# A conditioned attention and spatial-shift block on one core: the opening reordered, modulation loads issued by SyncE, shift-column loads in steps, two tail subtractions later

## The chip, the cores and the metric

The kernel runs on one core of one Trainium2 chip. The metric is the device time of one execution in microseconds (us), as the median of several runs. Runs of the same program differ by some tenths of a per cent. A core has five engines that work side by side, each through its own list of instructions in a fixed order: TensorE (PE: matmuls and transposes, with PEld for its weight loads), VectorE (DVE), ScalarE (ACT), GpSimd (POOL) and SyncE (SP, which here only issues DMA transfers). ScalarE can issue DMA transfers too. An instruction waits until what it reads is written and the buffer it writes is free; everything behind it on the same engine waits with it.

## The reference, cut to what matters

```python
def _A_ref(x, wqkv, wo):                      # S 2048, D 576, 32 heads of 18
    q, k, v = split(x @ wqkv)
    scores = einsum("bhqd,bhkd->bhqk", q, k) * 18 ** -0.5
    scores = where(0 <= query - key < 256, scores, -1e9)
    return merge(einsum("bhqk,bhkd->bhqd", softmax(scores), v)) @ wo

def _B_ref(x, w1, w2, w3, w4):                # F 4608
    h = gelu(layernorm(x) @ w1)
    hs = concat(four column groups of h, shifted by +1, -1, +2, -2 tokens) @ w2
    x1 = x + hs
    return x1 + gelu(layernorm(x1) @ w3) @ w4

sa, ca, ga, sb, cb, gb = six vectors of 576 from silu(c) @ w_mod
h = layernorm(x) * (1 + ca) + sa
x = x + ga * _A_ref(h, A_wqkv, A_wo)
h = layernorm(x) * (1 + cb) + sb
x = x + gb * _B_ref(h, B_w1, B_w2, B_w3, B_w4)
```

All data is fp32. Each of the six vectors `sa` to `gb` is called a modulation vector below; number 0 and 1 (`sa`, `ca`) are needed at the start, 2 to 5 later.

## The kernel before, in words

**Matmuls in two halves.** A matmul with full fp32 meaning is made of products of a high part (the value rounded to the fast matmul type) and a low part (what the rounding left). For an inner size of 576, four blocks of 128 and a tail of 64, that gives 14 matmuls for one result (`products`). So each operand is "split": one engine copies the high half, another subtracts it from the original for the low half.

**Stages.** The 2048 tokens lie in four groups of 512. Group by group their rows are normalised (`x_load`, `x_norm`), transposed to features by tokens (`x_tr`: transpose L373, scale and shift on ScalarE L380, high half on GpSimd L383, low half on VectorE L387; the result is `hT`) and multiplied by nine chunks of 128 columns of the q and k weights (`qk_item`, one "item" of 14 matmuls at L398, evicted by ScalarE L419, split by GpSimd L423 and L427) and by the V weights (`v_item`). The halves of q and k are stored to DRAM by SyncE (L435 to L441).

Attention runs in 32 units `u` of four heads and 512 queries. `pack(u)` loads a unit's q and k halves back from DRAM with twelve DMAs on SyncE (L475, L478) into one of three buffers (the third is called `big`), 1.6 units ahead. `scores(u)` makes a first set of score matmuls (L492) from which VectorE takes the row maxima (L499); they are transposed, copied by ScalarE (L518) and written by a DMA of ScalarE (L519) as two more rows of `Q`. `attend(u)` makes the scores again, transposed and with the maximum taken off (L539, and L548 for the mask), ScalarE's exponential (L558) into `P`, and the product with V (L569); the result is stored to the DRAM array `od` (L604).

While attention still runs, `s4a` does the output projection of the finished groups: it loads rows of `od` (L845) and x (L849), transposes them (L854), multiplies by `Wo` (L888), adds (VectorE, L893), normalises, and stores `xp`, `hbd`, `xnd` (L905). `load_w1` loads and splits five chunks of the mixer's first weights; one of them, `W14`, gathers sixteen columns from each of eight places, and its raw rows `W14r` come by twelve small DMAs (L975). `xnt0` transposes the first rows for the mixer: transposes L782, high halves by ScalarE (L785 and, for the 64-row tail, L796), low halves by VectorE (L789, tail L800). After attention the mixer and the channel MLP (L1380, L1426) follow; the change does not touch them.

**Later modulation vectors.** `modvec(v)` makes vector 2 to 5 in turn, in time units 2.7, 7.7, 12.7 and 17.7 and the five units after each. It loads five slices of 576 columns of `w_mod` by DMAs that ScalarE issues (L623), each one unit apart; GpSimd scales and adds them (L630, L632); a matmul with ones (L638) sums them over the partitions, and VectorE evicts the result (L641); SyncE stores it to the DRAM array `modd` (L644). All four vectors use one buffer `wm`, so the first load of a vector reuses what the store of the vector before reads.

**What sets the order.** `play(ev)` takes a list of pairs of time and step, and runs the steps by rising time. The times are written by hand, in units `u`; they only set the order in which instructions are emitted, and each engine keeps that order. Negative times are the opening, before unit 0.

**The opening.** `warm` issues matmuls on zeros (L269). `c_load` and `cond` make silu of the condition; `wm_load` loads the five slices of `w_mod` for vectors 0 and 1 (SyncE, L263), `mod_sum` multiplies them (L278), and `mod_row`, `mod_tr`, `mod_col` turn the result into columns. `w_load` loads a chunk of q and k weights `wr` (L306, with two DMAs for the tail in `load_dup`, L116 and L117), `w_split` splits it (ScalarE L313 and L314, VectorE for the low half). `clear` and `vones` are memsets of Q, K and V buffers by GpSimd.

Of the kernel before, what the change touches and what calls it, by code (L numbers as in the profile page):

```python
# [9 lines left out]
F32 = mybir.dt.float32  # L10
F32R = mybir.dt.float32r
BF16 = mybir.dt.bfloat16
AF = mybir.ActivationFunctionType
# [40 lines left out]
class Kern:  # L54
# [134 lines left out]
    def phase_a(self):  # L189
# [10 lines left out]
        with ExitStack() as st:  # L200
# [18 lines left out]
            def clear(i):  # L219
                nc.gpsimd.memset(Q[i].bitcast(F32), 0.0)  # L220
                nc.gpsimd.memset(K[i][96:128].bitcast(F32), 1.0)
# [76 lines left out]
            def w_load(c):  # L298
                def f():
                    raw = kp.tile([P, 1024], F32, tag="P", name=f"wr{c}", bufs=7)[:, 0:640] if c in (0, 4, 5, 1) else row(f"wr{c}")  # L300
# [3 lines left out]
                    if c == 0:  # L304
                        nc.vector.memset(raws[c][0:1, 0, 0:1], 0.0)
                    nc.sync.dma_start(raws[c][:, 0:KC, :], self.wqkv[0:KC * P, cs].rearrange("(k p) f -> p k f", p=P))  # L306
# [3 lines left out]
            def w_split(c, t, lo):  # L310
# [9 lines left out]
                return [(t, hi), (t + self.g_w, low)]  # L320
# [43 lines left out]
            def x_tr(g, k, t0):  # L364
# [3 lines left out]
                def tr():  # L368
                    if k == 0:
                        hT[g] = gp.tile([P, 2 * KC + 1, 512], F32R, tag="L", name=f"hT{g}", bufs=1)  # L370
                    pa = box["p"] = ps([P, 4, P], ("tr", "mm", "tr", "mm", "tr")[k] if g else ("mm", "tr", "av", "sc", "st")[k], f"hT{g}_{k}")
# [3 lines left out]
                def ev():  # L375
# [4 lines left out]
                    nc.scalar.activation(h[:n], box["p"][:n].rearrange("p a b -> p (a b)"), AF.Identity, bias=sa[:n, k:k + 1], scale=ca[:n, k:k + 1])  # L380
# [10 lines left out]
                return [(t0, tr), (t0 + 0.02, ev), (t0 + 0.055, hi), (t0 + 0.105, lo)]  # L391

# [221 lines left out]
            def modvec(v):  # L614
                acc = []

                def load(k):
                    def f():
# [4 lines left out]
                        nc.scalar.dma_start(acc[1 if k == 0 else 2][:kk], self.w_mod[k * P:k * P + kk, v * D:(v + 1) * D])  # L623
# [23 lines left out]
                return e + [(4.5 + 0.07 * hf + d, f) for hf in range(2) for d, f in bcast(hf)]  # L647
# [41 lines left out]
            wt = {0: -8.975, 4: -8.974, 5: -8.973, 1: -8.7, 6: -7.45, 2: -1.9, 7: -1.5, 3: -1.2, 8: -0.9}  # L689
            first = {0: (-8.2, -8.0), 4: (-7.95, -7.75), 5: (-7.7, -7.5), 1: (-2.08, -1.75), 6: (-1.08, -0.98), 2: (0.05, 0.4), 7: (0.9, 1.2), 3: (1.35, 1.65), 8: (1.8, 2.1)}  # L690
            ev = [(-9.5, warm(24)), (-9.45, consts), (-9.44, vones(0, 4)), (-9.405, c_load), (-9.2, wm_load), (-9.05, cond)]
            ev += [(-8.93, lambda: clear(1)), (-7.35, lambda: clear(2)), (-1.2, vones(4, 10))]
# [828 lines left out]
```

## Time and profile before

| | |
|---|---|
| runs of the kernel before | 1704.92, 1705.19 and 1711.11 us, median 1705.19 us |
| the profiled execution | 1705.17 us, with a span of 1703.4 us on the core and a mean granted TensorE clock of 0.993 |
| DMA | 283.04 MB in 160767 packets, 166 GB/s on average |
| costliest line | L1426, the last matmuls of the channel MLP: 440.7 us in 3036 matmuls, with 0.0 us idle before them |
| row maxima on VectorE (L499) | 270.8 us in 512 instructions of 544 ns on average |
| exponentials on ScalarE (L558) | 217.1 us in 384 instructions of 571 ns on average |

The profile is of one execution. A row of a trace list reads: start in us from the beginning of the span, length in us, engine, line, operation, output<-input by the program's names, and in brackets the idle time just ahead of it with what ended it (`<-ACT P L558` is the instruction of ScalarE at line 558 that writes or frees `P`). `SPq` and `ACTq` are the queues of SyncE and ScalarE in which DMA issues stand; the length of such a row is the time that the issue took. `xN` stands for N instructions in a row. A row of the list of waits reads: engine, what it wants, line, the releaser, then total us, number and the longest. A row of a window reads: from and to, length, then busy us and number of instructions of PE, PEld, DVE, ACT and POOL, the granted clock (1.00 is full speed), the DMA engines' busy share and GB/s.

### The profile page before, as it was taken

The page shows a single profiled execution, that of the slowest core. Times are in us where ns is not written, and L with a number is a line of the kernel's source. Part 1 is how long each engine was busy: PE and PEld are TensorE (multiplying, and loading weights), DVE is VectorE, ACT ScalarE, POOL GpSimd, SP SyncE. Part 2 cuts the span into 40 slices and gives each one's busy share as a digit, 9 for nine tenths or more (in the row PEclk, how much of TensorE's full clock was granted, in tenths as well). Part 3 has the DMA queues.
Part 4 walks back from the last instruction along what each step waited for, and adds up shares of the span by engine and source line. Part 5 has one row for each costly group of instructions (what it writes and reads, how often), then busy time and mean ns, then how long its engine had stood idle before and what let it go on. Part 6 is the DMA issues. An engine that isn't in the chain of part 4 may idle for free.

```text
span 1703.4 us, 30698 instructions
## 1 busy us (share of the span) xinstructions
PE 1648.5 (97%) x11103; PEld 1428.6 (84%) x11103; DVE 1176.5 (69%) x2527; ACT 710.0 (42%) x1324; POOL 803.8 (47%) x790
## 2 busy tenths in 40 slices
PE   8999899999998999999999999999999999999999
PEld 5777688777777787888999999999999999999998
DVE  5665565665676774777787888888875666666667
ACT  3354354554555665534244344343434222222221
POOL 6323232231335553134188888888864333323335
PEclk8999999999999999999999999999999999999999
DMA  7644545534557774544455655556565544455443
GB/s 201 204 125 148 137 122 139 151 110 121 146 161 195 194 199 144 186 127 139 145 193 189 223 203 195 177 208 225 207 218 185 173 157 139 135 170 173 136 137 110
DMA packets 160767, 283.04 MB, mean 166 GB/s; under 512 B 37988, under 2 KB 77412, under 8 KB 160616
## 3 DMA queue, kind: packets, MB, share of 16 engines
q1 hardware_dynamic: 157672, 275.24, 51.9%
q10 hardware_dynamic: 2944, 5.83, 1.3%
q8 instruction: 88, 1.44, 0.4%
q14 instruction: 63, 0.52, 0.1%
HBM read 168.71 MB, written 111.63 MB: 165 GB/s over the span
## 4 chain that ended last, share of the span: by engine, by line
PE 81%; DVE 6%; DMA 6%; POOL 3%; ACT 2%; issue 1%; SPq 1%; ACTq 0%; POOLq 0%; DVEq 0%
PE pall L1380 27%; PE pall L1426 24%; PE pall L398 8%; PE pall L569 4%; PE pall L539 4%; PE pall L492 4%; PE pall L548 2%; PE pall L811 2%; PE pall L888 2%; PE pall L1164 2%; DVE pall L499 1%; DMA Q<-ms 1%; DMA wr<-in_A_wqkv_dram 1%; PE pall L580 1%; DMA modd<-wm 0%
## 5 line engine op out<-in xcount | busy, mean ns | idle before, releaser
L1426 PEld LDWEIGHTS pall<-W,G 128*128 128x128 f32 x3036 | 428.3, 188 | 19.2
L1426 PE MATMUL pall<-W,G 128*128 128x288 f32 x3036 | 440.7, 294 | 0.0
L499 DVE CUSTOM_DVE_ANT_0 pall<-pall,mask 128x384 f32<-128x384 f32 (+2 forms) x512 | 270.8, 544 | 194.9 <-PE pall L492 191.8
L1380 PE MATMUL pall<-LNT,W 128*128 128x512 f32 x1512 | 374.8, 390 | 0.0
L1435 DVE TENSOR_TENSOR accA<-pall,accA 128x576 f32<-128x576 f32 (+1 forms) x337 | 254.1, 756 | 120.8 <-PE pall L1426 109.3
L1351 POOL TENSOR_TENSOR g<-g,g 128x512 f32<-128x512 f32 x140 | 185.6, 1326 | 292.3 <-DVE G L1346 150.1
L1380 PEld LDWEIGHTS pall<-LNT,W 128*128 128x128 f32 x1512 | 274.7, 188 | 45.5
L558 ACT ACTIVATE P<-pall 128x512 f32<-128x512 f32 (+2 forms) x384 | 217.1, 571 | 180.8 <-PE pall L548 160.4
L1343 ACT CAST G<-g 128x512 fp32r<-128x512 f32 x249 | 151.1, 621 | 271.7 <-POOL g L1351 269.9
L1346 DVE TENSOR_TENSOR G<-g,G 128x512 fp32r<-128x512 f32 x249 | 240.7, 968 | 11.5 <-ACT G L1343 11.4
L1384 ACT ACTIVATE g<-pall 128x512 f32<-128x512 f32 x144 | 85.9, 596 | 194.3 <-PE pall L1380 184.7
L1435 DVE TENSOR_TENSOR accB<-pall,accB 128x576 f32<-128x576 f32 x134 | 101.3, 757 | 91.1 <-PE pall L1426 89.1
L398 PE MATMUL pall<-hT,Wc 128*128 128x512 f32 x504 | 158.8, 416 | 3.7 <-POOL hT L383 1.6
L423 POOL CAST qe<-qe 128x512 fp32r<-128x512 f32 x36 | 22.7, 630 | 244.8 <-ACT qe L419 232.4
L492 PE MATMUL pall<-K,Q 108*128 108x384 f32 (+2 forms) x352 | 125.7, 368 | 2.3 <-DVE m L499 0.8
L1380 PE MATMUL pall<-big,W 128*128 128x512 f32 x504 | 126.2, 390 | 0.0
L548 PE MATMUL pall<-maskb,identb 128*128 128x256 bf16 (+1 forms) x640 | 121.0, 255 | 0.0
L539 PE MATMUL pall<-Q,K 110*128 110x384 f32 (+1 forms) x480 | 105.7, 293 | 6.0 <-DMA Q<-ms 3.1
L1380 PEld LDWEIGHTS pall<-big,W 128*128 128x128 f32 x504 | 90.9, 188 | 14.1
L539 PEld LDWEIGHTS pall<-Q,K 110*128 110x128 f32 x480 | 86.3, 192 | 19.1 <-issue 6.1
L398 PEld LDWEIGHTS pall<-hT,Wc 128*128 128x128 f32 x504 | 86.7, 192 | 16.7 <-issue 3.3
L398 PE MATMUL pall<-Wv,hT 128*128 128x288 f32 x448 | 83.8, 311 | 2.7 <-ACT qe L419 2.7
(679 smaller groups left out, 2399.8 us busy)
## 6 DMA issues: line engine op xcount, KB each, us to landing
w4d<-W SPq DMA_DIRECT2D x55, 576.0 KB
W<-w4d SPq DMA_DIRECT2D x55, 576.0 KB
w3d<-W SPq DMA_DIRECT2D x36, 640.0 KB
W<-w3d SPq DMA_DIRECT2D x36, 640.0 KB
r<-in_B_w_dram SPq DMA_DIRECT2D x36, 288.0 KB
K<-k0d SPq DMA_DIRECT2D x64, 108.0 KB
Q<-q0d SPq DMA_DIRECT2D x88, 72.0 KB
w4d<-W SPq DMA_DIRECT2D x17, 288.0 KB
```

The source lines that it names most:

```text
L398: nc.tensor.matmul(pm, pl()[i][0], pl()[i][1], start=(i == 0), stop=(i == 13))
L492: nc.tensor.matmul(sc[:, lo:], q[0:2 * R3, h, i * P:(i + 1) * P], k[0:2 * R3, h // 2, i * P + lo:(i + 3) * P], start=True, stop=True)
L499: nc.vector.tensor_tensor_reduce(out=sc[:, lo:], in0=sc[:, lo:], in1=mask[:, lo:], scale=1.0, scalar=-3e38, op0=ALU.add, op1=ALU.max, accu ...
L539: nc.tensor.matmul(x[:, p0 * P:(p0 + w) * P], k[0:2 * R3 + 2, h // 2, (kb + 2) * P:(kb + 3) * P], q[0:2 * R3 + 2, h, q0 * P:(q0 + w) * P], ...
L548: nc.tensor.matmul(x[:, p0 * P:(p0 + w) * P], self.identb, m, start=False, stop=(n == len(ms) - 1))
L558: nc.scalar.activation(pt[:, c0:c1, h % 2, :], x[:, c0 * P:c1 * P].rearrange("p (a b) -> p a b", b=P), AF.Exp, scale=SCALE)
L1343: nc.scalar.copy(T[:, 0], src())
L1346: nc.vector.tensor_tensor(out=sp[m][:, 1], in0=src(), in1=sp[m][:, 0].bitcast(F32), op=sub)
L1351: nc.gpsimd.tensor_tensor(out=g[o] if o in g else gt(o), in0=g[a], in1=g[b], op=op)
L1380: nc.tensor.matmul(box["p"], box["l"][i][1], box["l"][i][0], start=(i == 0), stop=(i == 13))
L1426: nc.tensor.matmul(po, a, b, start=(n == 0), stop=(n == len(seq) - 1))
L1435: nc.vector.tensor_tensor(out=ac, in0=po, in1=ac, op=ALU.add)
```

## The change

It has five parts.

1. *Opening.* 36 instead of 24 warm-up matmuls. The transposes of the first group's rows are issued row by row (`x_tr0(i)`: the five blocks of row i), between the `mod_sum` steps, instead of block by block after them; scaling and splitting stay by block. The split of weight chunk 0 moves behind the first block's high half, and its low half follows it with a lag of 0.002. Chunk 4's load gets a wait: ScalarE copies one element of the fourth slice of the modulation weights into its buffer first, so that it (and chunk 5 behind it) starts when that slice is there. Chunks 6 and 2 get buffers of the `P` kind and are loaded right behind chunk 1, not among the q and k stores and loads. The last two products of item 0 (chunk 0) are put late, behind the first six of item 4. The clears of the second and third Q and K buffers, and six of the memsets of V, come later.
2. *Modulation loads.* `modvec`'s loads are issued by SyncE instead of ScalarE, and everything of `modvec` starts 0.6 units earlier, the summing matmul 0.05 of a unit more.
3. *Shift columns.* The twelve DMAs of `W14r` come in five steps 0.2 of a unit apart: pairs for the four blocks of 128 rows, four DMAs for the tail. The split of all five W1 chunks stands 1.2 units after the first DMA instead of 0.8 (`w1_d`).
4. *Tail low halves.* In `xnt0` the low halves by VectorE come at 0.17 and 0.21 instead of 0.1 and 0.16.
5. The lag of `w_split` becomes an argument, with the same default of 0.05.

What stands in ScalarE's order around the first load of the second later vector (`wm` is its buffer, `avs` an eviction of `attend`), before:

```order
L558 ACTIVATE P_0_0_2138<-pall 128x4x128 x2
L574 COPY avs_2184<-pall 128x512
L558 ACTIVATE P_0_2_2186<-pall 128x4x128
L623 DMA wm_2195<-in_w_mod_dram 128x576
L558 ACTIVATE P_0_2_2186<-pall 128x4x128
L419 COPY qe_3_2206<-pall 128x512
```

And the same load in SyncE's order, with the change (L623 is now the store to `od`, L663 the store to `modd`, L642 the modulation load, L458 and L460 k stores, L494 and L497 the loads of a unit's q and k):

```order
L623 DMA od_129<-o_2031 128x4x72
L663 DMA modd_133<-wm_1133 1x576
L642 DMA wm_2086<-in_w_mod_dram 128x576
L458 DMA k0d_147<-qe_7_2070 128x512
L460 DMA k0d_149<-qe_7_2070 128x256
L458 DMA k1d_148<-qe_7_2070 128x512
L460 DMA k1d_150<-qe_7_2070 128x256
L494 DMA Q_170<-q0d_139 18x2x512
L497 DMA K_172<-k0d_147 18x2x768
```

The load has left ScalarE's exponentials; on SyncE it stands right behind the store that it waits for, with four stores of k and the next unit's twelve loads behind it.

SyncE's order at the loads of the shift columns, before:

```order
L604 DMA od_131<-o_5647 128x4x72
L975 DMA W14r<-in_B_w_dram 128x4x16 x4
L975 DMA W14r<-in_B_w_dram 64x4x16 x2
L975 DMA W14r<-in_B_w_dram 128x4x16 x4
L975 DMA W14r<-in_B_w_dram 64x4x16 x2
L849 DMA s4rows<-in_A_x_dram 128x576
L905 DMA hbd_81<-or_5300 128x576
L475 DMA big<-q0d_143 18x2x512
```

With the change:

```order
L623 DMA od_131<-o_5660 128x4x72
L1005 DMA W14r<-in_B_w_dram 128x4x16 x2
L873 DMA s4rows<-in_A_x_dram 128x576
L1005 DMA W14r<-in_B_w_dram 128x4x16 x2
L929 DMA hbd_81<-or_5318 128x576
L1005 DMA W14r<-in_B_w_dram 128x4x16 x2
L494 DMA big<-q0d_143 18x2x512
```

Six of the twelve stand ahead of the unit's loads now, two of them behind the store of `hbd`; the other six follow behind the unit's loads.

VectorE's order in the tail of attention, before and then with the change (`big` holds the transposed rows for the mixer there, L893 and L917 are the add of the output projection, L789 and L812 the large low half, L800 and L823 that of the 64-row tail):

```order
L143 SCALAR_TENSOR_TENSOR b10rs<-b10mv,b10rs 128x1
L789 TENSOR_TENSOR big<-pall,big 128x4x128
L800 TENSOR_TENSOR big<-pall,big 64x128
L893 TENSOR_TENSOR s4rows<-pall,s4rows 128x288
L789 TENSOR_TENSOR big<-pall,big 128x4x128
L800 TENSOR_TENSOR big<-pall,big 64x128
```

```order
L143 SCALAR_TENSOR_TENSOR b10rs<-b10mv,b10rs 128x1
L812 TENSOR_TENSOR big<-pall,big 128x4x128
L917 TENSOR_TENSOR s4rows<-pall,s4rows 128x288
L823 TENSOR_TENSOR big<-pall,big 64x128
L812 TENSOR_TENSOR big<-pall,big 128x4x128
```

The add has passed the first of the 64-row pieces; the large piece still stands ahead of it.

The diff, cut to what the text above and the prediction speak of:

```diff
-                    raw = kp.tile([P, 1024], ..., name=f"wr{c}", bufs=7)[:, 0:640] if c in (0, 4, 5, 1) else row(f"wr{c}")
+                    raw = kp.tile([P, 1024], ..., name=f"wr{c}", bufs=7)[:, 0:640] if c in (0, 4, 5, 1, 6, 2) else row(f"wr{c}")
...
+                    if c == 4:
+                        nc.scalar.copy(raws[c][0:1, 0, 0:1], wm["t"][0:1, 3, 0:1])
...
-                return [(t, hi), (t + self.g_w, low)]
+                return [(t, hi), (t + lag, low)]
...
-                    a, b = (-8.92 + 0.001 * k, -8.84 + 0.01 * k) if k < KC else (-8.82, -8.79)
-                    return [(a, tr), (b, ev), (b + 0.001, hi), (b + 0.021, lo)]
+                    b = -8.84 + 0.01 * k if k < KC else -8.79
+                    return [(b, ev), (b + 0.001, hi), (b + 0.021, lo)]
...
+            def x_tr0(i):
+                def f():
+                    if i == 0:
...
+                    for k in range(KC + 1):
+                        n = P if k < KC else TAIL
+                        nc.tensor.transpose(h0["p"][k][:n, i, :], xrows[i][:, k * P:k * P + n], self.ident)
+                return f
...
-                        nc.scalar.dma_start(acc[1 if k == 0 else 2][:kk], self.w_mod[k * P:k * P + kk, v * D:(v + 1) * D])
+                        nc.sync.dma_start(acc[1 if k == 0 else 2][:kk], self.w_mod[k * P:k * P + kk, v * D:(v + 1) * D])
...
-                return e + [(4.5 + 0.07 * hf + d, f) for hf in range(2) for d, f in bcast(hf)]
+                return e + [(4.45 + 0.07 * hf + d, f) for hf in range(2) for d, f in bcast(hf)]
...
-            wt = {0: -8.975, 4: -8.974, 5: -8.973, 1: -8.7, 6: -7.45, 2: -1.9, 7: -1.5, 3: -1.2, 8: -0.9}
+            wt = {0: -8.975, 4: -8.955, 5: -8.954, 1: -8.7, 6: -8.69, 2: -8.68, 7: -1.5, 3: -1.2, 8: -0.9}
...
-            ev = [(-9.5, warm(24)), ...]
-            ev += [(-8.93, lambda: clear(1)), (-7.35, lambda: clear(2)), (-1.2, vones(4, 10))]
+            ev = [(-9.5, warm(36)), ...]
+            ev += [(-7.4, lambda: clear(1)), (-1.65, lambda: clear(2)), (0.6, vones(4, 7)), (1.3, vones(7, 10))]
...
-            ev += [(-8.95 + 0.01 * k, mod_sum(k)) for k in range(3)] + [(-8.91 + 0.001 * k, mod_sum(3 + k)) for k in range(2)]
+            ev += [(t, mod_sum(k)) for k, t in enumerate((-8.95, -8.94, -8.93, -8.91, -8.909))]
+            ev += [(t, x_tr0(i)) for i, t in enumerate((-8.936, -8.934, -8.928, -8.92))]
...
-            ev += w_split(0, -8.9, ...) + w_split(4, -8.3, ...) + w_split(5, -8.1, ...)
+            ev += w_split(0, -8.835, ..., 0.002) + w_split(4, -8.795, ..., 0.01) + w_split(5, -8.1, ...)
...
-                ev += put(qk_item(0, c, kinds.get(c, "mm")), *first[c])
+                ev += put(qk_item(0, c, kinds.get(c, "mm")), *first[c], -7.85 if c == 0 else None)
...
-                ev += [(2.7 + 5.0 * n + d, f) for d, f in modvec(v)]
+                ev += [(2.1 + 5.0 * n + d, f) for d, f in modvec(v)]
...
-        return [(t0, tr), (t0 + 0.06, hi), (t0 + 0.1, lo), (t0 + 0.07, trt), (t0 + 0.13, hit), (t0 + 0.16, lot)]
+        return [(t0, tr), (t0 + 0.06, hi), (t0 + 0.17, lo), (t0 + 0.07, trt), (t0 + 0.13, hit), (t0 + 0.21, lot)]
...
+        def part(k):
+            sv = src.rearrange("d (q f) -> d q f", q=4)[:, :, P:]
+            n = P if k < KC else TAIL
+            for u in range(2):
+                for r0 in ((0,) if k < KC else (0, TAIL)):
+                    nc.sync.dma_start(box["r"][r0:r0 + n, k, :]..., sv[k * P:k * P + n])
...
-            return [(t, begin), (t + 0.8, hi), (t + 0.85, lo)]
+            e = [(t, begin), (t + self.w1_d, hi), (t + self.w1_d + 0.05, lo)]
+            return e + [(t + 0.2 * k, more(k)) for k in range(1, KC + 1) if fc == KC]
```

More of the change, by code (lines that the diff above doesn't have):

```diff
@@ L705, in phase_a, with put @@
                 ev += v_split(k, -7.98 + 0.07 * k)
[L707 removed]
+            def put(it, t0, t1, late=None):
                 steps, evac = it
[L709 removed]
+                e = spread(steps, t0, t1)
+                if late is not None:
+                    e[-1], t1 = (late, steps[-1]), late
+                return e + [(t1 + d, f) for d, f in evac]
             kinds = {0: "mm", 4: "av", 5: "mm", 1: "av", 6: "mm", 2: "av"}
             for c in order:
[L713 removed]
+                ev += put(qk_item(0, c, kinds.get(c, "mm")), *first[c], -7.85 if c == 0 else None)
             vt = [-2.6, -2.35, -1.6, -1.3, -0.6, -0.3, 0.45, 0.65]
@@ L988, in lo @@
             l(out=w[:, 2 * KC + 1, :], in0=r[:, KC, :], in1=w[:, 2 * KC, :].bitcast(F32), op=ALU.subtract)
-        return load, hi, lo
+        return load, hi, lo, part
     def load_w1(self, t0, dt):
@@ L1001, in begin, with more, f @@
                     self.W1[fc] = load()
-            return [(t, begin), (t + 0.8, hi), (t + 0.85, lo)]
+            def more(k):
+                def f():
+                    with nc.allow_non_contiguous_dma("sixteen columns of a shift group"):
+                        part(k)
+                return f
+            e = [(t, begin), (t + self.w1_d, hi), (t + self.w1_d + 0.05, lo)]
+            return e + [(t + 0.2 * k, more(k)) for k in range(1, KC + 1) if fc == KC]
         return [e for n, fc in enumerate((KC, 0, 1, 2, 3)) for e in one(fc, t0 + dt * n)]
```

36 lines of the change are left out of this document (19 added, 17 removed).

## The prediction

> **What bounds the kernel now.** I read the head of the page first, then the waits of TensorE, then the granted clock around the longest of them, and only then the timeline at each place that the diff touches.
>
> ```profile
> span 1703.4 us, 30698 instructions
> PE 1648.5 (97%) x11103; PEld 1428.6 (84%) x11103; DVE 1176.5 (69%) x2527; ACT 710.0 (42%) x1324; POOL 803.8 (47%) x790
> ```
>
> TensorE is busy for 97% of the span and no other engine for over 69% (its weight loads overlap). The diff removes no matmul that the result needs, so it can gain only from TensorE's idle time, 1703.4 - 1648.5 = 54.9 us, and from stretches at a lower clock. The waits of TensorE (total, times, longest) say who causes the idle time:
>
> ```profile
> PE pall L539 <- ACT P L558: 5.9, 7, 2.0
> PE pall L492 <- DMA od<-o: 3.3, 1, 3.3
> PE pall L398 <- ACT qe L419: 3.3, 3, 2.7
> PE pall L854 <- DMA s4rows<-od: 3.2, 1, 3.2
> PE pall L888 <- DVE s4rows L893: 2.5, 3, 1.9
> ```
>
> A few single waits make most of it. Some also cost clock: the windows below (the last but two of the columns is the granted clock) are four stretches of 3.4 us at 0.50.
>
> ```profile
> 51.50:54.90 3.40, 3.40 (x17) 3.40 (x16) 1.77 (x9) 0.00 (x0) 0.00 (x0) 0.50 0.52 163
> 181.20:184.60 3.40, 3.40 (x18) 3.28 (x17) 1.39 (x5) 1.34 (x3) 0.09 (x1) 0.50 0.04 15
> 532.80:536.20 3.40, 3.40 (x19) 3.03 (x18) 3.07 (x10) 1.77 (x4) 2.46 (x4) 0.50 0.99 291
> 659.10:662.50 3.40, 3.40 (x18) 3.29 (x17) 1.77 (x5) 1.19 (x3) 0.80 (x3) 0.50 0.57 174
> ```
>
> TensorE is busy all through each, at half rate: 3.4 x 0.5 = 1.7 us of work lost in each. Each begins 1 to 4 us after a wait that the change touches (at 48.8, 176.6, 528.4 and 655.7). I count the 1.7 us with the wait.
>
> **Modulation loads: ScalarE's hold.** The first load of each later vector reuses the buffer that the store of the vector before still reads, so the load waits for that store. It stands in ScalarE's order, and what is behind it waits too.
>
> ```profile
> 191.82 0.23 SPq L644 DMA_DIRECT2D modd<-wm  x1
> 194.11 0.60 ACT L558 ACTIVATE P<-pall 128x512 f32<-128x512 f32 x1 [0.46 <-PE pall L548]
> 198.14 0.33 ACTq L623 DMA_DIRECT2D wm<-in_w_mod_dram  x1
> 198.51 0.60 ACT L558 ACTIVATE P<-pall 128x512 f32<-128x512 f32 x1 [3.80 <-DVE m L499]
> 393.13 1.08 ACT L558 ACTIVATE P<-pall 128x512 f32<-128x512 f32 x2 [3.40 <-DMA modd<-wm]
> 199.64 0.53 PE L398 MATMUL pall<-Wv,hT 128*128 128x288 f32 x2 [2.70 <-ACT qe L419]
> 292.92 0.50 PE L539 MATMUL pall<-Q,K 110*128 110x384 f32 x2 [1.13 <-ACT P L558]
> 393.78 0.50 PE L539 MATMUL pall<-big 110*128 110x384 f32 x2 [2.03 <-ACT P L558]
> ```
>
> From 194.71 to 198.14 ScalarE does nothing though an exponential and an eviction are ready; the row at 198.51 names DVE, which had long been done. The store at 191.82 was only past at 198.14, 6.3 us later. TensorE pays 2.70, and at the two other changes of vector 1.13 and 2.03: 5.86 us. With the load on SyncE, ScalarE goes on. Ends: 0 (TensorE meets another wait at once) and -5.86. I take **-5.0**, near the full end, since VectorE and GpSimd, next in line, are busy 69% and 47%.
>
> **Modulation loads: SyncE's stall.** Each of 20 loads is placed on ScalarE, but transfers of both queues pass in one order, a few at a time, and SyncE can be held by a load that ScalarE issues late.
>
> ```profile
> 170.42 0.57 ACTq L623 DMA_DIRECT2D wm<-in_w_mod_dram  x1
> 170.54 0.27 SPq L478 DMA_DIRECT2D big<-k0d  x1
> 176.63 0.27 SPq L475 DMA_DIRECT2D big<-q0d  x1
> 176.94 0.32 SPq L478 DMA_DIRECT2D big<-k1d  x1
> 179.90 0.41 PE L492 MATMUL pall<-big 108*128 108x384 f32 x1 [3.32 <-DMA od<-o]
> SPq L435 <- DMA wm<-in_w_mod_dram: 18.5, 6, 5.5
> ```
>
> Two of the twelve loads of a unit's q and k are held for 6.1 us by the modulation load, land about 3 us after 176.94, and TensorE stands for 3.32; with the half clock, 5.0 us. The last row shows that this hold is usual (18.5 us at one line) but mostly hidden. In the changed order SyncE issues the load itself, and mostly before the unit's loads, so it is on its way when they come. Ends: 0 and -5.0; I take **-4.0**.
>
> What is added: 20 issues of 0.33 us (row at 198.14) make 6.6 us on SyncE over some 380 us, beside its idle time. SyncE also takes over ScalarE's wait, up to 6.3 us at three places, with k stores and the next unit's twelve loads queued behind it. How much may it be late? At 170.54 it was late by 176.63 - 170.54 less a normal 0.36, 5.7 us, and TensorE lost 3.32, so 2.4 us are covered. Three waits at worst cost 3 x (6.3 - 2.4) = 11.7 us, at best nothing; the unit's loads are due about a third of a unit later, so I take **+2.0**.
>
> **Shift columns in five steps.** The twelve loads of sixteen-column pieces stand in one block on SyncE.
>
> ```profile
> 509.17 8.29 SPq L975 DMA_DIRECT2D W14r<-in_B_w_dram  x12
> 512.72 1.44 POOL L902 TENSOR_TENSOR or<-or,sb 128x576 f32<-128x576 f32 x1
> 518.69 0.29 SPq L475 DMA_DIRECT2D big<-q0d  x1
> 525.18 0.35 SPq L845 DMA_DIRECT2D s4rows<-od  x1
> 531.60 0.66 PE L854 MATMUL pall<-ident,s4rows 128*128 128x128 f32 x4 [3.18 <-DMA s4rows<-od]
> ```
>
> At 8.29 / 12 = 0.69 us each, six stay ahead of the unit's loads and six go behind: 4.1 us less. But the store of `hbd` among them needs GpSimd's result of 512.72 + 1.44 = 514.2; with the last pair behind it the loads start at about 515.6, 3.1 us sooner than 518.69, and the `od` row with them. That covers the 3.18 us but for a rest, and the 1.7 us of clock goes too. The other six, 4.1 us, lie among SyncE's idle times behind. The split of these weights moves 0.4 of a unit later, long before its matmuls. Ends 0 and -4.9; I take **-4.0**.
>
> **Tail low halves later.** VectorE's order at the end of attention:
>
> ```profile
> 655.41 0.69 DVE L789 TENSOR_TENSOR big<-pall,big 128x512 fp32r<-128x512 f32 x1 [2.80 <-ACT big L785]
> 656.80 0.28 DVE L800 TENSOR_TENSOR big<-pall,big 64x128 fp32r<-64x128 f32 x1 [0.70 <-ACT big L796]
> 657.12 0.46 DVE L893 TENSOR_TENSOR s4rows<-pall,s4rows 128x288 f32<-128x288 f32 x1
> 657.63 0.81 PE L888 MATMUL pall<-Wo,oT 128*128 128x288 f32 x4 [1.93 <-DVE s4rows L893]
> ```
>
> The add that frees TensorE's bank now stands ahead of the 64-row piece. It can start when the large one ends, 655.41 + 0.69 = 656.10, so 657.12 - 656.10 = 1.02 us sooner. A wait of 0.9 us remains. With a gap that short I take the 1.7 us of clock as saved: **-2.7**. Ends: 0, if the large low half is late too, and 1.93 + 1.7 = -3.6.
>
> The Trainium skill (TensorE: Matmul & The Clock Gate, Part 1) has the clock fall to half after at least one idle window of about 3.4 us. The trace differs: half clock follows 1.93 us here and 0.81 at 48.8. By the page only the waits of 3.32 and 3.18 could cost clock, and the sum would end 1.7 us higher.
>
> **Opening.**
>
> ```profile
> 13.18 2.03 DVE L160 TENSOR_SCALAR x<-x,a3mv,a3rs 128x576 f32<-128x576 f32 x1 [0.97 <-POOL a3rs L138]
> 18.97 0.15 PEld L278 LDWEIGHTS pall<-wm,silub 64*32 64x32 f32 x8 [0.52 <-DMA wm<-in_w_mod_dram]
> 22.88 0.73 PE L398 MATMUL pall<-hT,Wc 128*128 128x512 f32 x2 [1.57 <-POOL hT L383]
> 39.85 0.41 SPq L306 DMA_DIRECT2D wr<-in_A_wqkv_dram  x1
> 46.36 0.40 SPq L306 DMA_DIRECT2D wr<-in_A_wqkv_dram  x1
> 49.59 0.54 PE L492 MATMUL pall<-K,Q 108*128 108x128 f32 x3 [0.81 <-DMA wr<-in_A_wqkv_dram]
> ```
>
> Transposes row by row, twelve more warm-up matmuls and a faster norm (13.18 ran beside the clear that moves away) all end before the last slice of modulation weights, whose arrival at 18.97 sets the start of real work at 22.88. They gain nothing by themselves; without that cover the transposes would count. Holding weight chunks 4 and 5 until the fourth slice is there brings this arrival forward, but the split of chunk 0 now stands ahead of the first low half on VectorE and the second `h` on ScalarE, about 0.9 us, and the held chunks and V weights land later. Ends +3 and -3; I take **0**.
>
> Two weight chunks leave SyncE's chain ahead of the first k loads (39.85) and the second unit (46.36), three issues of 0.4 us or more each, at least 1.2 us per chunk, where TensorE waits 0.81 and then loses clock. Against it, item 0's eviction is put later. Ends 0 and -2.5; **-1.5**.
>
> **Sum**, against the profiled execution of 1705.17 us (span 1703.4 and 1.8 around it; the median of the runs is 1705.19): -5.0 - 4.0 + 2.0 - 4.0 - 2.7 + 0 - 1.5 = -15.2, so **1690.0 us**. All good ends together give -24.9, 1680.3.
>
> **The rivals.**
> *The waits return elsewhere.* The order of 4,200 rows on TensorE is fixed, and behind each wait stands the next: VectorE's maximum, the row of maxima by DMA, the exponentials. For it: small waits of 0.3 to 0.9 us on such releasers fill the list after the long ones. Against it: 69% on VectorE. If 60% of the gain is lost, 1705.2 - 6 = 1699.
> *SyncE becomes the bound (slower).* A modulation load now stands in the same queue ahead of a unit's twelve loads. Place: the unit's first score matmul. Price: as at 179.90, 5.0 us for a unit whose loads are held 5.7 us. It decides if it happens in more than about four of 20 units: the other terms give some -14, five units pay +25, so 1716 and up; six, 1721. For it: SyncE is held often already. Against it: the load comes earlier in the unit, and lands while SyncE still waits.
> The Trainium skill (DMA: Bandwidth & Descriptors, Queues, rings and completion order) speaks for this rival: SyncE and ScalarE own a row of rings each, served in turn, and within a row descriptors go in ring order. By that rule the load goes whole ahead of q and k. No run here shows it yet.
> *Everything at its good end.* Also the opening gains 3 us: 1676 to 1684.
>
> **How the numbers follow.** Forecast (1684 to 1697) 0.60, waits return 0.22, SyncE bound 0.09, all good 0.09. 0.5% is 8.5 us, about what a measurement of this kernel can tell from no change: faster than 1696.7 are the first, the last and a little of the second, 0.72; within are most of the second, 0.19; slower 0.09. The range 1680 to 1703 leaves out the last 0.09 and the lowest few hundredths. Its upper end keeps the second case, its lower end the good ends.
>
> **What would show it.** Right: no idle ScalarE of 3 us ahead of an exponential near 195, 289 and 390; no wait of TensorE over 2 us from 60 to 640 us; clock 1.00 near 181, 533 and 659; no block of SyncE of 8 us. Wrong: TensorE waiting for q or k loads or rows of maxima behind a modulation load on SyncE; first real matmul later than 23; a new wait of several us where one went.

## The result, and the profile after

The changed kernel takes 1685.98 us (median of 4 runs, 1684.02 to 1688.36), the kernel before 1706.06 us beside it (4 runs). The ratio is 0.9877, with a 95% interval of 0.9853 to 0.9901: faster by 20.1 us. (The ratio, here and below, is the one that was recorded with the runs; it is not the quotient of the two medians, which is 0.9882.) One execution of the kernel before, beside the experiments, took 3216.32 us and is left out everywhere. The forecast was 1690.0 in a range of 1680 to 1703. The profiled execution took 1684.02 us, 21.15 less than that of before. The head of its page and the top of TensorE's list of waits (total, times, longest):

```profile
span 1682.2 us, 30737 instructions
PE 1644.7 (98%) x11115; PEld 1425.8 (85%) x11115; DVE 1165.1 (69%) x2527; ACT 709.4 (42%) x1325; POOL 804.0 (48%) x790
```

```profile
PE pall L558 <- ACT P L577: 4.1, 6, 1.5
PE pall L558 <- DMA Q<-ms: 3.5, 2, 3.2
PE pall L912 <- DVE oT L899: 2.0, 5, 0.6
PE pall L417 <- ACT Wc L322: 1.9, 1, 1.9
PE pall L511 <- DMA xr<-in_A_x_dram: 1.8, 1, 1.8
```

Span less busy time, TensorE is idle for 37.5 us instead of 54.9. Its busy time fell by 3.8 us though twelve matmuls were added: that is clock (the mean granted clock is 0.996 instead of 0.993). The wait for `od` (L492 before, 3.3), that for `qe` (L398, 3.3 in all), that for `s4rows` (L854, 3.2) and the longest on the add (L888, 1.9) are gone from the top. Three entries are new in kind or size: a wait of 3.2 for a row of maxima, one of 1.9 for the split of a weight chunk in the opening, and one of 1.8 for rows of x that the output projection adds (`xr`).

Where the 21.15 us come from can be read by pairing each matmul with its counterpart, since TensorE's order behind the opening hardly changed. The difference of the two start times is flat between events and steps at them:

| start in the profile before | counterpart's shift there | step | what lies there |
|---|---|---|---|
| 45 | -1.40 | -1.40 | opening |
| 65 | -3.66 | -2.26 | wait at 48.8 and its half clock |
| 170 | -4.15 | -0.49 | small ones |
| 190 | -8.95 | -4.80 | wait of 3.32 and its half clock |
| 200 | -11.81 | -2.86 | ScalarE's hold, first change of vector |
| 300 | -13.22 | -1.41 | second change of vector |
| 385 | -15.69 | -2.47 | small waits near 338 to 342 (-1.7) and 361 (-0.9) |
| 400 | -17.80 | -2.11 | third change of vector |
| 476 | -14.26 | **+3.54** | row of maxima near 439 of the changed kernel |
| 520 | -14.89 | -0.63 | a wait of 1.3 at 477.6 gone, the new one of 1.8 |
| 545 | -15.79 | -0.90 | shift columns |
| 640 | -17.73 | -1.94 | split of the mixer's first weights |
| 665 | -20.41 | -2.68 | tail low halves |
| 800 | -21.18 | -0.77 | small ones |

Behind 800 the shift stays between -21.1 and -21.2. The step from 545 to 640 is put to the split of the first weights since the kernel with that part alone has most of it too (below). Two thirds of it, 1.4 us, lie at two places where GpSimd's subtraction for such a split ran beside VectorE's two small steps ahead of a row of maxima, before:

```profile
573.60 1.27 POOL L987 TENSOR_TENSOR W<-W13r,W 128x512 fp32r<-128x512 f32 x1
573.71 1.19 DVE L506 SCALAR_TENSOR_TENSOR mr<-m,mr 128x16 fp32r<-128x16 f32 x1
```

The two steps took 0.72 and 0.38 us at the first place and 1.04 and 1.19 at the second; in the changed kernel, where the splits stand elsewhere, they take 0.17 and 0.18, then 0.17 and 1.28.

The windows of the changed kernel at the counterparts of four places of half clock (51.5, 181.2, 532.8 and 659.1 of before) and at two new ones; the granted clock is the last column but two:

```profile
50.00:53.40 3.40, 3.40 (x26) 3.25 (x25) 2.80 (x10) 1.12 (x3) 0.16 (x1) 1.00 0.67 160
172.40:175.80 3.40, 3.33 (x25) 2.80 (x25) 2.33 (x10) 2.42 (x5) 1.78 (x2) 1.00 0.33 80
516.60:520.00 3.40, 1.45 (x9) 0.82 (x7) 1.32 (x5) 1.37 (x4) 3.24 (x6) 1.00 0.80 200
638.70:642.10 3.40, 3.30 (x27) 3.19 (x28) 1.66 (x5) 2.65 (x7) 2.65 (x2) 1.00 0.00 0
442.10:445.50 3.40, 3.40 (x15) 2.72 (x14) 1.58 (x5) 1.20 (x2) 3.40 (x4) 0.58 0.59 145
520.20:523.60 3.40, 2.99 (x14) 2.93 (x15) 2.17 (x10) 3.14 (x5) 0.32 (x1) 0.64 0.87 252
```

The old places run at 1.00, though the third of them now holds idle time (TensorE busy for 1.45 of 3.40). The two new ones each follow a new wait. The timeline of the changed kernel shows the first:

```profile
432.81 0.38 SPq L673 DMA_DIRECT2D ga<-modd  x1
433.28 0.41 SPq L693 DMA_DIRECT2D wor<-in_A_wo_dram  x1
433.74 0.50 SPq L642 DMA_DIRECT2D wm<-in_w_mod_dram  x1
434.33 1.48 SPq L693 DMA_DIRECT2D wor<-in_A_wo_dram  x3
435.73 0.62 ACTq L538 DMA_DIRECT2D Q<-ms  x1
441.93 0.47 PE L558 MATMUL pall<-Q,K 110*128 110x384 f32 x2 [3.19 <-DMA Q<-ms]
```

The row of maxima, 16 KB, is issued at 435.73 behind six loads of 144 to 288 KB, one of them now the last modulation slice, and TensorE has it at 441.93. The second new wait stands at the shift columns:

```profile
513.54 2.82 SPq L1005 DMA_DIRECT2D W14r<-in_B_w_dram  x4
515.47 0.61 ACT L1008 CAST W<-W14r 128x512 fp32r<-128x512 f32 x1
517.92 0.30 ACT L1009 CAST W<-W14r 128x128 fp32r<-128x128 f32 x1 [1.84 <-DMA W14r<-in_B_w_dram]
518.12 0.59 ACT L577 ACTIVATE P<-pall 128x512 f32<-128x512 f32 x1
518.76 0.50 PE L558 MATMUL pall<-Q,K 110*128 110x256 f32 x2 [1.52 <-ACT P L577]
520.61 0.86 PE L912 MATMUL pall<-Wo,oT 128*128 128x288 f32 x4 [1.04 <-POOL b2rs L138]
```

The last four DMAs of `W14r` are issued until 516.36. ScalarE's copy of their rows stands in its order already and waits 1.84 us for them, with a ready exponential behind it; TensorE waits 1.52 for that. On GpSimd the low half of the same weights stands ahead of the root of a variance (`b2rs`), which makes the 1.04.

### The profile page after: what moved, and what is told of

It is laid out like the page before. It is cut to its first block, busy times and chain, and to the rows that moved or that the text cites. A ratio compares the mean times of both kernels' runs of the same rounds, so it can differ in the third digit from the quotient of the medians.

```text
span 1682.2 us, 30737 instructions
## 1 busy us (share of the span) xinstructions
PE 1644.7 (98%) x11115; PEld 1425.8 (85%) x11115; DVE 1165.1 (69%) x2527; ACT 709.4 (42%) x1325; POOL 804.0 (48%) x790
## 4 chain that ended last, share of the span: by engine, by line
PE 86%; DVE 5%; DMA 3%; POOL 2%; ACT 2%; issue 1%; SPq 1%; ACTq 0%; POOLq 0%; DVEq 0%
PE pall L1413 27%; PE pall L1459 24%; PE pall L417 10%; PE pall L588 4%; PE pall L558 4%; PE pall L511 4%; PE pall L567 3%; PE pall L912 2%; PE pall L834 2%; PE pall L1197 2%; DVE pall L518 1%; PE pall L599 1%; DMA wm<-in_w_mod_dram 1%; DMA Q<-ms 1%; DMA wr<-in_A_wqkv_dram 1%
## 5 line engine op out<-in xcount | busy, mean ns | idle before, releaser
L588 PE MATMUL pall<-P,V 128*32 128x384 f32 (+2 forms) x1408 | 84.4, 387 | 0.0
```

The costliest lines, as they stand in the source:

```text
L588: nc.tensor.matmul(abox[0][32 * h:32 * h + 32, q0 * P:(q0 + w) * P], v[:, hh * VA:hh * VA + 32], Pt[b, h // 2][:, p0:p0 + w, h % 2, :], st ...
```

## The experiments

Twelve kernels ran in three groups: each part alone on the kernel before, then the two new waits on the changed kernel, then what in the parts works. Ratios are to the kernel before on the same chip (its median 1707.98, 1710.13 and 1708.22 in the three groups; 25 runs of it in the first lie between 1702.37 and 1712.85). A gain in us behind a ratio is worked out from the ratio. "Local" is the step of the paired start times at a place.

**Each part alone**

The modulation loads (with the summing matmul at 4.45 instead of 4.5):

```diff
-   nc.scalar.dma_start(acc[1 if k == 0 else 2][:kk], ...)
+   nc.sync.dma_start(acc[1 if k == 0 else 2][:kk], ...)
-   (2.7 + 5.0 * n + d, f) for d, f in modvec(v)
+   (2.1 + 5.0 * n + d, f) for d, f in modvec(v)
```

> Only the modulation loads are changed (issued by SyncE, 0.6 units earlier). Theory: the waits at 176.6 (3.32, with the half clock behind it), 196.9 (2.70), 291.8 (1.13) and 391.8 (2.03) go, 4.8 + 6.4 us, and a few short ones between 317 and 385 (about 2.5 us); the row of maxima near 456 (1.70 before) waits longer, since the last slice now falls among the loads of Wo, and costs 3.5 us more. Together -10 us: 1695 to 1697, and alone it shows the wait of over 3 us near 446. Rival: these waits go only together with the earlier weight loads of the opening, or the wait near 446 comes from another part: then 1699 or more, or 1693 and less without a wait of 3 us there.

Measured: 1697.09, ratio 0.9926 [0.9911, 0.9941], so -12.6 us. Local: -4.8 near 176, -2.9, -1.4 and -2.0 at the changes of vector, -2.5 from 300 to 385, and +3.7 near 444, where this kernel has a wait of 3.13 for the row of maxima. The theory holds with its loss. This part is about three fifths of the whole gain.

The shift columns (the steps, and the split at 1.2 instead of 0.8):

```diff
-   return [(t, begin), (t + 0.8, hi), (t + 0.85, lo)]
+   e = [(t, begin), (t + self.w1_d, hi), (t + self.w1_d + 0.05, lo)]
+   return e + [(t + 0.2 * k, more(k)) for k in range(1, KC + 1) if fc == KC]
```

> Only the loads of the shift columns come in steps, with the split 1.2 units behind the first. Theory: the wait of 3.18 at 528.4 goes with its half clock (-4.9), but ScalarE's split of these weights now stands only 0.4 units behind the last four loads and waits for them, which holds the exponentials and, through GpSimd's part of the split, the next root of a variance: new waits of 1.5 and 1.0 us with a half clock, so -0.5 to -1.5 us in all, 1704 to 1705.5. Rival: the new waits near 517 of the changed kernel come from another part or from chance in DMA times; then this kernel keeps the full gain of 4 us: 1701 to 1702.

Measured: 1705.91, ratio 0.9977 [0.9962, 0.9992], so -3.9 us with some 2.5 either way. The wait at the counterpart of 531.60 is gone, and a new one of 2.42 with half clock stands a few us behind it: +0.3 from 520 to 545 in all, then -2.0 up to 640 (the kernels with the tail or the modulation part alone have -0.2 and -0.5 there). The new wait belongs to this part. That the time is nearer to the rival's than to the theory's may come from the profile of before: its wait of 3.18 there was a short one. The same wait in the six other kernels here that keep the old column loads is 4.11 to 4.61 us, so there was about 1.2 us more to gain than I had read off.

The tail low halves (`lo` at 0.17 and `lot` at 0.21 in `xnt0`):

> Only the two tail low halves come later. Theory: the wait of 1.93 at 655.7 shrinks by 1.0 and the half clock behind it goes: -2.7 us, 1703 to 1703.5, with a granted clock of 0.95 or more from 657 to 663. Rival: the half clock stays, since the large low half is still ahead of the add: -1.0, and 0.50 in that stretch.

Measured: 1707.40, ratio 0.9999 [0.9985, 1.0013]. Local: -2.7, as expected; the wait is 0.81 and no half clock follows. But the whole kernel shows no difference; its interval, from -2.6 to +2.2 us, holds a gain of 1 to 2.6 us as well as none. The kernels that keep the old order say how much of the 2.7 to expect: all seven have the wait of 1.90 to 1.93, and behind it the clock drops in five profiles and not in two, those of the opening alone and of the modulation loads alone. The windows of the opening-only kernel there:

```profile
657.90:661.30 3.40, 1.47 (x12) 1.37 (x12) 1.88 (x4) 2.18 (x6) 2.76 (x2) 1.00 0.10 37
661.30:664.70 3.40, 3.40 (x40) 2.73 (x43) 2.34 (x7) 2.45 (x6) 0.84 (x3) 1.00 0.58 192
```

The same wait of 1.93 is followed by 1.00 here, and by 0.50 in the window 659.10 to 662.50 of the kernel before that the prediction shows. So 1.0 us is there in each of them, and the 1.7 of clock in some executions only.

The opening (part 1, nothing else):

> Only the opening is changed. Theory: -1.4 us by 40 us and another -2.2 us at 49 to 55, where two weight chunks are loaded earlier and the half clock goes: -3.6, 1702 to 1702.5, and nothing behind 60 us. Rival: the transposes by row and the extra warm-up gain by the kernel's start alone and the loads of the two chunks hold other loads up: then the delta is under 2 us at 60 us, or later units move.

Measured: 1704.68, ratio 0.9975 [0.9961, 0.9989], so -4.3 us. Local: -2.9 by 60 us, the larger part of it at 49 to 58, but in this profile +2.9 at 94 to 100 from a half clock that has nothing to do with the opening (see the last section).

The four parts alone give -12.6, -3.9, -0.2 and -4.3, together -21.0 us, where the whole has -21.0 by its ratio and -20.1 by its medians: they add, within intervals of some 2.5 us for each part. (By the plain medians the four come to -16.8.)

**The two new waits**

The changed kernel once more:

> The changed kernel unchanged, to stand beside the next three on the same chip: 1683 to 1688, with the waits of 3.2 for a row of maxima near 439 and of 1.5 and 1.0 near 517 to 520.

Measured: 1685.84, ratio 0.9863 [0.9838, 0.9888], with waits of 3.46 near 437 and 2.31 near 515.

The split of the shift columns later:

```diff
+   w1_d = self.w1_d + (0.4 if fc == KC else 0.0)
```

> The changed kernel with the split of the shift columns 1.6 units after their first load, not 1.2. Theory (ScalarE and GpSimd wait there for the last four loads): the waits of 1.52 and 1.04 near 517 to 520 and the half clock behind them go, 2.5 to 4 us less than the changed kernel. Rival (the waits are the exponentials' and the variance roots' own lateness, with the split only standing beside): they stay within 0.5 us and the time is the same.

Measured: 1685.66, ratio 0.9858 [0.9835, 0.9881]. The waits of 1.52 and 1.04 and their half clock are gone, -3.7 us locally. ScalarE's order shows why: the copies run late, as soon as they are reached and without a wait.

```profile
520.36 0.60 ACT L577 ACTIVATE P<-pall 128x512 f32<-128x512 f32 x1
520.86 0.61 ACT L1008 CAST W<-W14r 128x512 fp32r<-128x512 f32 x1
521.37 0.30 ACT L1009 CAST W<-W14r 128x128 fp32r<-128x128 f32 x1
533.27 0.41 PE L511 MATMUL pall<-K,Q 108*128 108x384 f32 x1 [1.47 <-DVE c2rs L143]
```

The cause of the waits is settled. But the last row is a new wait, 12 us later, which takes 1.2 us back; the time shows no difference that the runs resolve.

The last vector's slices closer together:

```diff
-   e = [(k + d, f) for k in range(KC + 1) ...]
+   e = [((0.9 if v == 5 else 1.0) * k + d, f) for k in range(KC + 1) ...]
```

> The changed kernel with the slices of the last modulation vector 0.9 units apart instead of 1.0, so that its fifth slice is issued some 18 DMAs ahead of the output weights' loads, not among them. Theory A (that slice delays the row of maxima): the wait of 3.2 near 439 falls to the 1.7 of before or less, with its half clock, 1.5 to 3.5 us less. Rival B (the four output-weight loads and the broadcast of the gate alone fill the queue): the wait stays at 2.5 to 3.2 and the time is the same.

Measured: 1684.32, ratio 0.9845 [0.9818, 0.9872]. The burst stands without the slice now, and the wait is halved:

```profile
435.95 0.38 SPq L673 DMA_DIRECT2D ga<-modd  x1
436.43 1.82 SPq L693 DMA_DIRECT2D wor<-in_A_wo_dram  x4
443.89 0.47 PE L558 MATMUL pall<-Q,K 110*128 110x384 f32 x2 [1.58 <-DMA Q<-ms]
```

No half clock follows, and the local step against the changed kernel is -2.7. Theory A holds: one slice of 144 KB among the output weights' loads made the difference between 1.6 and 3.2 to 3.5 us. The next kernel shows that theory A is not the whole of it.

The output weights' loads later, with the split at 1.6 as above:

```diff
-   (w1 - 1.7, wo_ga), ... wo_one(k, w1 - 1.65 + 0.1 * k)
+   (w1 - 1.45, wo_ga), ... wo_one(k, w1 - 1.4 + 0.1 * k)
```

> The changed kernel with the split of the shift columns at 1.6 units, and the loads of the gate and the output weights 0.25 units later, so that the next unit's loads stand among them and the row of maxima is issued ahead of three of them. By rival B of the run before, the wait near 439 falls under 1 us and the half clock behind it goes; with the waits near 517 gone too, 1677 to 1681, 4 to 7 us less than the changed kernel. By theory A the wait stays near 3 and only the 2.5 to 4 us of the split show.

Measured: 1684.98, ratio 0.9858 [0.9836, 0.9879]: a miss. The wait near 439 is gone altogether, a local -5.0, so thinning the burst in this way works as well, as rival B had it for this kernel: it isn't that slice as such that counts, but how much SyncE has issued ahead of the row. But the kernel gives back 4.7 within 25 us, and of the 3.7 that the later split brings near 517 another 3.5 near 537:

```profile
461.91 0.51 PE L558 MATMUL pall<-Q,K 110*128 110x256 f32 x2 [1.35 <-ACT P L577]
464.71 0.79 PE L417 MATMUL pall<-hT,Wc 128*128 128x512 f32 x2 [1.04 <-ACT qe L438]
537.27 0.66 PE L511 MATMUL pall<-K,Q 108*128 108x384 f32 x1 [2.37 <-DMA W12r<-in_B_w_dram]
```

**What in the parts works**

The change of queue and the earlier time of the modulation loads, each alone:

> The kernel before with the modulation loads issued by SyncE at their old times (2.7 units, right behind a unit's twelve loads). Theory: it is the engine that counts. ScalarE is not held, so the waits of 2.7, 1.1 and 2.0 at the changes of vector go (-6 us), and the wait of 3.3 near 177 goes too, since the load passes with SyncE's own order (-4.8): 1695 to 1698. Rival: the place counts as much; at the old time SyncE's waits for the store fall on the q stores and the next unit's loads, and the wait near 177 stays or moves: 1700 to 1704.

> The kernel before with the modulation loads still issued by ScalarE, but 0.6 units earlier. Theory: ScalarE is still held by the store of the vector before, so three waits of TensorE of 1 to 3 us for an exponential or an eviction stay (at the changes of vector, some 11 us earlier), and SyncE is still held by loads that ScalarE issues late: -3 us at most, 1703 to 1709 on this chip. Rival: the earlier place alone makes the gain, and this kernel comes to 1696.

Measured: the queue alone 1696.85, ratio 0.9929 [0.9914, 0.9945]; the earlier time alone, still on ScalarE, 1699.16, ratio 0.9941 [0.9925, 0.9957]. The theory that only the engine counts fell. Near 176 the steps are -3.8 and -4.8, at the three changes of vector -2.9, -1.4, -2.3 and -2.9, -1.4, -2.3. Either edit alone takes both faults away. The timelines at the first change of vector, first of the kernel with the queue changed alone, then of the one with the earlier time alone:

```profile
190.41 0.23 SPq L644 DMA_DIRECT2D modd<-wm  x1
191.04 0.36 SPq L349 DMA_DIRECT2D x<-in_A_x_dram  x1
196.21 0.35 SPq L623 DMA_DIRECT2D wm<-in_w_mod_dram  x1
```

```profile
178.74 0.23 SPq L644 DMA_DIRECT2D modd<-wm  x1
180.48 0.33 ACTq L623 DMA_DIRECT2D wm<-in_w_mod_dram  x1
450.17 0.76 PE L539 MATMUL pall<-Q,K 110*128 110x384 f32 x2 [4.98 <-DMA Q<-ms]
```

At the old place the store takes some 5.8 us until the load can go, between loads of x rows; SyncE then stands instead of ScalarE, and nothing on TensorE feels it. At the earlier place store and load are 1.7 us apart and ScalarE is hardly held. The last row shows the price of the earlier place: the last slice falls into the burst near 440, and 6.5 us are lost there (a wait of 4.98 and half clock). The queue alone, at the old time, loses 0.2 us in that stretch. What the earlier time adds is most of the -2.5 us between 300 and 385 (the queue alone has -0.7 there). As a whole the three versions can't be told apart by their times.

Of the opening, the early loads of weight chunks 6 and 2 alone (`c in (0, 4, 5, 1, 6, 2)`, and -8.69 and -8.68 in `wt`):

> The kernel before with weight chunks 6 and 2 loaded early into other buffers, and nothing else of the opening changed. Theory: the wait of 0.81 at 48.8 and the half clock at 51.5 to 54.9 go: -2.3 us by 60 us, nothing behind it. Rival: the gain there comes from the opening's shifted start or from the clears that moved: under 1 us here.

Measured: 1706.62, ratio 0.9986 [0.9973, 0.9999]. Locally -2.3 us between 45 and 65, and the wait of 0.8 at the first score matmuls is gone. This gain is that of the two chunks: in all eight profiles with the early loads the clock stays at 1.00 from 45 to 56, and in five of the six with the old loads it falls to 0.50 there. (Four of the 14 profiles have a half clock between 56 and 65 instead or besides, two of them with the early loads; it costs them some 1.7 us.) The rest of the opening can be read from all profiles by their shift at 40 us: the seven with the old opening stand between -1.1 and +1.0 there (mean -0.1), the seven with the new one between -2.2 and -0.2 (mean -1.3).

The two single edits together:

> The changed kernel with both single edits that paid: the split of the shift columns at 1.6 units, and the last vector's slices 0.9 units apart. The two act at different places (near 439 and near 517), so their 2.7 and 2.5 us should add: some 5 us less than the changed kernel, 1679 to 1682. Rival: as with the later output-weight loads, what is gained near 439 is given back by the next wait within 40 us: 1682 to 1685.

Measured: 1684.45, ratio 0.9850 [0.9830, 0.9869]. The local gains of -2.7 and -3.7 are both there, and +3.2 comes back near 535 with a wait of 1.95 for a store of `hbd` and its half clock. Its interval overlaps that of the changed kernel: no version here beats it by what the runs can tell.

## Why the prediction was right, point by point

The sign, the places and the order of size were right; the gain was 20.1 where the sum said 15.2. That it came out past the sum and not short of it is partly luck: the shift columns gained less and the new wait cost more than was priced, and a term that the sum left out (-2.5) and four terms that came out past their prices outweighed both. One of the signs of being right failed: a wait of 3.19 us stands near 439, where none over 2 us was to be. By its steps:

- **Modulation loads, ScalarE's hold (-5.0).** Measured -6.4 in three steps, past its good end by half a us: each step is 0.1 to 0.3 more than the wait itself. The fault was read rightly: an exponential that stands behind a load that waits for a store. The other queue, which the step names as the cure, isn't needed: the earlier place cures it too.
- **SyncE's stall (-4.0).** Measured -4.8, the half clock included, as at its good end. The trace bears the reading out: the DMAs of both queues take eight completion semaphores in turn, and the load at 176.63 was issued just as the last piece of the modulation load of 170.42, which had the same semaphore, landed. The hold that the prediction calls usual but mostly hidden was not hidden between 300 and 385: -2.5 us more came there, the largest item that the sum left out. Some -1.7 of it is one such hold, of 5.4 us, of loads of x rows in the kernel before; VectorE's normalisation of these rows comes late, and the row maxima that stand among it:

```profile
SPq L349 <- DMA wm<-in_w_mod_dram: 5.4, 1, 5.4
331.70 1.30 SPq L349 DMA_DIRECT2D x<-in_A_x_dram  x3
338.29 0.44 PE L492 MATMUL pall<-K,Q 108*128 108x384 f32 x1 [0.62 <-DVE m L499]
```

  The other -0.9, near 361, was not taken apart.
- **New waits on SyncE (+2.0).** Measured +3.5, at one place. The mechanism was not the one that I priced: not SyncE standing for the store (it stood 5.8 us in one kernel and nothing followed), but one more load in a burst, which delays a small DMA of ScalarE. The prediction had named the place among its signs of being wrong (rows of maxima behind a modulation load on SyncE), but gave it no price. The rival that SyncE becomes the bound did not come; the same kernels show that SyncE had room.
- **Shift columns (-4.0).** Measured -0.9 there and -1.9 behind, of which some -1.4 is this part's. This is the step that failed. "The split of these weights moves 0.4 of a unit later, long before its matmuls" looked at the matmuls that read the result and not at the loads that the split waits for. The last four loads moved by 0.8 of a unit, the split by 0.4 only, so the split came closer to its data and held ScalarE and GpSimd. The numbers for it were in the change itself: the last loads at 4 x 0.2 = 0.8 of a unit, the split at 1.2.
- **Tail low halves (-2.7).** Measured -2.7 in the profile: 637.69 + 0.69 for the large half, the add at 638.30, and a wait of 0.81 in place of 1.93. Run alone the time doesn't resolve it, and the clock's 1.7 is there in five of the seven profiles with the old order only: 1.0 is sure, the rest depends on the execution.

```profile
637.69 0.69 DVE L812 TENSOR_TENSOR big<-pall,big 128x512 fp32r<-128x512 f32 x1 [2.79 <-ACT big L808]
638.30 0.45 DVE L917 TENSOR_TENSOR s4rows<-pall,s4rows 128x288 f32<-128x288 f32 x1
638.80 0.79 PE L912 MATMUL pall<-Wo,oT 128*128 128x288 f32 x4 [0.81 <-DVE s4rows L917]
```

- **Opening (0).** Measured -1.4, inside its ends. The split of chunk 0 ahead did become late, as feared:

```profile
16.98 0.74 PE L284 MATMUL pall<-wm,silub 64*32 64x320 f32 x8 [0.61 <-DMA wm<-in_w_mod_dram]
20.82 3.73 PE L417 MATMUL pall<-hT,Wc 128*128 128x512 f32 x6 [1.93 <-ACT Wc L322]
```

  The last slice comes 2 us earlier (16.98 against 18.97), and the first real matmul at 20.82 instead of 22.88 in spite of a wait of 1.93 for that split. The means of seven and seven profiles above say that some 1.2 us of it are the opening's.
- **Weight chunks off SyncE's chain (-1.5).** Measured -2.3, alone too; near its good end, with the half clock gone.
- **"Waits return elsewhere"** came true in small: +3.5 and the 2.6 us of waits at the shift columns. And it is what stopped each attempt to go further.

The Trainium skill (TensorE: Matmul & The Clock Gate, Part 1) says that the window in which activity is measured runs freely, so that the point at which the clock changes varies from run to run. The runs agree: one wait of 1.93 us, with and without a drop, and a raster of 3.41 us that lies elsewhere in each execution (next section but one). Its idle window of about 3.4 us ahead of a drop is not what these runs show, where drops follow waits of 0.8 to 1.9 us too.

## What to carry to other kernels

When a load is split into later steps, move its consumer by as much as its last piece, and look at who stands behind that consumer on its engine. A wait for a slow store can be cured by its place as well as by its queue: look at what is ahead of the store first. And where many small waits stand in a fixed order, price each edit by its local step, and expect the next wait to take back a part of it.

## What was not expected of the hardware

**The same waits, with and without a drop of the clock.** In all kernels of this study TensorE has a wait of 0.90 and one of 0.81 us, 1.4 us apart, near 95 us. In 9 of 14 profiles the clock falls to 0.50 for 3 to 7 us behind them and costs 1.6 to 2.9 us; in the others, the kernels before and after among them, it stays. The waits in the timeline of the opening-only kernel, and then its windows there:

```profile
92.32 0.38 PE L558 MATMUL pall<-Q,K 110*128 110x256 f32 x1 [0.90 <-ACT P L577]
93.75 0.76 PE L558 MATMUL pall<-big 110*128 110x384 f32 x2 [0.80 <-DMA big<-ms]
```

```profile
93.50:95.20 1.70, 1.45 (x7) 1.39 (x8) 0.09 (x1) 0.30 (x1) 0.00 (x0) 0.50 0.77 269
95.20:96.90 1.70, 1.70 (x10) 1.61 (x9) 1.02 (x4) 1.07 (x2) 0.09 (x1) 0.50 0.42 123
```

The traces say what decides. In each profile all stretches of half clock begin and end on one raster of 3.41 us, which lies elsewhere in each execution. Take the cells of this raster at full clock, from 30 to 1500 us of all 14 profiles. Behind a cell in which TensorE was busy for less than 0.45 of the time, the next one is at 0.50 in 26 of 26 cases; behind one with 0.75 or more, in none of 5795; between, in 25 of 132. Where the raster lets both waits near 95 us fall into one cell (busy for 0.50 of it), the clock falls in six profiles of six; the wait of 1.93 in the tail left cells of 0.43 to 0.45 in the five profiles with a drop and of 0.49 and 0.51 in the two without. (The busy shares are worked out from the matmul rows, whose ends are modelled.)

One profile of a kernel with many short waits is therefore uncertain by a few us in the clock alone; the profile of before happened to lie 2.8 us under the median of 25 runs of it.

**A small DMA behind a full burst.** The 16 KB row of maxima, issued on ScalarE's own queue, took 6.2 us from its issue to the matmul that waited for it, while SyncE's loads kept the DMA engines busy:

```profile
436.00:439.00 3.00, 2.74 (x21) 2.38 (x19) 1.71 (x7) 2.12 (x4) 0.00 (x0) 1.00 1.03 258
439.00:442.00 3.00, 0.07 (x1) 0.10 (x1) 0.40 (x2) 0.00 (x1) 2.72 (x3) 1.00 1.01 247
```

The page of the changed kernel has that queue apart, with little in it:

```profile
q10 hardware_dynamic: 320, 0.52, 0.1%
```

A queue of its own did not let it pass: the DMA engines' busy share is 1.0 in both windows, and one load less in the burst halved the wait. The packets of that queue show where the time went. The first of the row's ten moves 4.5 us after the issue, when nine tenths of what SyncE had issued before it have moved, and all are through 0.4 us later. Without the slice the first moves after 3.1 us, with three of the output weights' loads behind the row after 1.3 us, which is also the median of the 32 rows of the changed kernel.
